# Six, then eight buffers for attention's exponentials, wo's maximum by a matrix product, wo's inputs by halves into one lasting tile, and a new order of all steps

## The chip, the cores and the metric

One core of a Trainium2 chip runs the whole program. The time is the device time of one execution in microseconds; the number compared is the median over runs. Before the change it is 800.88 us (three runs: 796.53, 800.88 and 806.01).

The core's engines work through their own instruction streams in order and meet at semaphores: PE (matrix products; PEld is its weight loading), DVE (vector), ACT (activations), POOL, and SP, which here only issues DMA transfers.

## The reference

Two independent results are joined along the last axis. A is windowed attention with 32 heads of 18 features, 2048 positions and a window of 256. B is a state-space convolution: a kernel of 2048 taps for each of 576 channels is formed from 128 complex modes, and convolved with u.

```python
def _A_ref(x, wqkv, wo):                     # x [1,2048,576]
    q, k, v = split((x @ wqkv), heads=32, Dh=18)
    scores = einsum("bhqd,bhkd->bhqk", q, k) * 18 ** -0.5
    mask = (idx[:, None] - idx[None, :] >= 0) & (idx[:, None] - idx[None, :] < 256)
    p = softmax(where(mask, scores, -1e9))
    return einsum("bhqk,bhkd->bhqd", p, v).concat_heads() @ wo

def _B_ref(u, A_re, A_im, B_re, B_im, C_re, C_im, log_dt, Dskip):
    dt = exp(log_dt)[:, None]
    P = exp((dt * A)[:, :, None] * arange(2048))      # A = A_re + 1j*A_im
    K = einsum("dn,dnl,dn->dl", Cc, P, dt * Bc).real
    return irfft(rfft(pad(u.T)) * rfft(pad(K)))[:2048].T + u * Dskip

return concatenate([a, b], axis=-1)
```

## The kernel before

**The order is a table.** Every piece of work is a Python generator (a stream) whose steps each issue a few instructions. `run` reads the strings of `PLAN` from left to right: a letter advances that stream by one step, a letter with a digit issues an evacuation, a conversion or a store that an earlier step of that stream has posted. So `PLAN` alone sets the order of instructions on every engine and on SP's queue. The conditions that the generators yield beside their steps play no part when the program is built. There are four strings: `front` (loads, scales, the first projections), `tables` (projections, the taps of B, transforms of u and of the taps), `first` (the last taps beside the first attention blocks), and `rest` (attention, convolution, output projection).

**PSUM.** All work but the projections and the products P times V takes its PSUM tile from `slot()`: the string `SLOTS` names, allocation by allocation, one of three ring buffers of two banks. A ring buffer comes free when the evacuation that reads it has run.

**Attention** has 16 items (4 chunks of 512 queries times 4 groups of 8 heads). For each item `smax1` forms the scores on PE (L901 the product, L909 and L912 the mask) and takes row maxima on DVE (L935); 16 reductions for each item. The maxima are transposed (L917, L921) and written by DMA into row 54 of Q (L928). `scores` and `score1` form the scores again, transposed, with the maximum taken off (L971, mask L984). ACT takes the exponential into an SBUF tile P of 128x2x512 (L989). `pv` multiplies P by V (L1009) into the PSUM tile `po`. An item has 5 blocks of keys, and a block needs two P tiles, so there are 160 exponentials. The pool `P` has 4 buffers: the fifth exponential waits until the products that read the first are done.

**Normalizing.** ACT copies `po` to `osb` (L1019). DVE transposes, takes reciprocals and transposes back (L1035, L1037, L1039). POOL multiplies (L1044), ACT makes the high half in f16 (L1048), POOL the low half (L1052), and SP stores both to the DRAM tensor `od` (L1057).

**The output projection.** `wo_load` fetches wo in four column pieces, reduces each to its maximum over the row (DVE L1081), then needs the maximum over all 128 partitions: `om` is stored to a row of DRAM (L1088), loaded back to all partitions as `orow` (L1090), and reduced there (L1092, result `og`). From it come the scales `so` and `osc` (L183 to L187 and L1095). `wo` loads one chunk of 512 positions at a time as f16 high and low tiles `oh` and `ol` (8 DMAs, L1117 and L1118) from a pool with one buffer each. Then come 8 groups of 14 matmuls (L203; ring tiles read woh, wol, oh and ol), and the result is scaled (ACT L1132, tile `ya`, two buffers) and stored (L1133).

**The convolution** in `rest`: loads of spectra parts (L705), forward products (L717), ACT copies (L725), DVE products (L732), POOL sums (L738, L739), inverse products (L750), stores and loads through `h` (L757, L763, L802), last products (L813) and outputs (ACT L820, store L824).

**Memory.** The pool `rawp` has 8 tiles of 128x5x256 f32. They first hold the eight pieces of x. `early` then reuses six of them as Q, K and V of the first two items; two tiles lie idle after that, and so do the two K tiles once the first two items have their scores.

Of the kernel before, what the change touches and what calls it, by code (L numbers as in the profile page):

```python
# [10 lines left out]
F32 = mybir.dt.float32  # L11
F16 = mybir.dt.float16
# [30 lines left out]
def constants():  # L43
# [23 lines left out]
    for nm, v in mult.items():  # L67
# [34 lines left out]
        "PMP6RP5XP5X4P6XG6ssM1RNX2NsssRssMss2s2X1sU4X5s2ssZss2ss2Zsss2s2XX1X4s2s2Zss2Rs2s2Xs2X5Zs2s2",
    "first":
        "Rs2ssMs6M1Rss4s2sss2X2as2aa1X4Ma1s2XRss2sXX1s2sX1sXsas2vsaX5a1s2sa1X2X4svs2as2vs2X4ssavaX4sX4a1as2ss"
        "2s2a1avs2s2sa1svsassa1s6s2s2sss2s2a1s",
    "rest":
        "s2sa1ssvvsss2vs2ss2s4ssvas2av1kss2as2as2a1s2ka1a1s2a1s2vcknvLc1s2skaLaaa1vs6a1ks4vcc2svka1lkc1slsasv"
        "kas2saa1a1s2vs2s2c2avcs2sks2sas2a1sn3a1ss2vc1sLs2vc3a1aLdv1s2Lsc3a1c2csds2d1svlsaas2kvc1c2s2cd1a1s2s"
        "sLka1d4nc3vc1s2d4ks2vaa1aslsasvas6s2svs2dLsas4a1a1svs2c2c3a1d1c3ss2sa1n1vks2aa1svasdsLss2n6a1s2vv1s2"
        "Las2svd1a1n3saslvLs2ls2ss2s2kasa1s2s2lcs2ssn1sa1s6s2das2c1a1vsLcc2d1c1vaas2nvssa1d4n6c3laks4a1sava1s"  # L110
        "s2vavss2s2a1kss2vs2vsn3s2adas2sa1csv1d4d4a1svsn4d1c2s2aa1ss2vc3s2s2ac1dss2aa1c2a1d1vvks2Lc3nsa1Ln1aL"
        "dsd4a1vkd1n3sass6s2s2va1sasn4va1d4sad4s2sa1s2vcss4s2vkLss2saaan6fsc1s2sa1vfLss2ea1s2skLs2s2vs2sas2va"
        "1c2v1s2c3ase1Lds2s2a1e4a1sls6n1ss2ssvsavksasd1ss2a1fvksaa1svaas4s2La1va1fs2kcvs2s2n4a1s2slavsc1s2s2a"
        "1asnLa1vsas2s2kaLv1s2c2vva1n6cLsa1ssleas2c1fave1vs2s2s2se4a1kaacs6a1a1vvaa1c2ss4ac1nvssLvsas2s2c3sa1"
# [1143 lines left out]
```

## Time and profile before

| what | value |
|---|---|
| median of 3 runs | 800.88 us |
| the profiled execution | 799.52 us |
| its span in the trace | 797.8 us |
| mean granted PE clock | 0.974 |
| PE busy | 693.7 us (87%) |
| DVE busy | 601.7 us (75%) |
| ACT busy | 534.1 us (67%) |
| POOL busy | 369.2 us (46%) |
| DMA | 150.74 MB, mean 189 GB/s |

Times in the trace are counted from the start of the span; 1.7 us of the execution lie outside it. The strings of `PLAN` can be told apart by which lines run: the projections end near 355 us, the taps near 387 us, the first product P times V is at 389.5 us, and the last one ends at 756.6 us. After that only the output projection and the last products of the convolution are left.

### The profile page before, as it was taken

To read this page: it belongs to the slowest core of one execution; us is meant where nothing else is said; L and a number is where in the kernel's file an instruction comes from. 1 tells how busy PE (TensorE), PEld (TensorE's weight loads), DVE (VectorE), ACT (ScalarE), POOL (GpSimd) and SP (SyncE) were. 2 spreads that over 40 slices of the span, in tenths; PEclk is the share of its full clock that TensorE was granted. 3 is DMA by queue.
4 is the path that set the end of the run, shared out by engine and by line. 5 is a ranking of instruction groups with operands and counts; after the bars stand their busy time and mean duration, and the time that the engine had idled before them with its cause. 6 is when DMAs were issued, how large, how long until landed. Compare 5 with 4: busy or idle time off the path is not lost.

```text
span 797.8 us, 29495 instructions
## 1 busy us (share of the span) xinstructions
PE 693.7 (87%) x12954; PEld 406.1 (51%) x12954; DVE 601.7 (75%) x803; ACT 534.1 (67%) x709; POOL 369.2 (46%) x285
## 2 busy tenths in 40 slices
PE   3775889988889989987888999988999998999986
PEld 2532445455445645655544555544545555466655
DVE  5898988988898898778788988867888788851010
ACT  2279677787876787773466677765777868775422
POOL 2236967886789667676022433230342242443120
PEclk9989899999999999996899999999999999999999
DMA  8978256348336727887669677778566797636574
GB/s 300 369 166 203 64 129 168 83 104 216 83 75 173 166 54 185 221 210 217 162 196 313 208 219 225 203 178 275 157 201 221 232 284 227 177 112 199 185 241 156
DMA packets 211072, 150.74 MB, mean 189 GB/s; under 512 B 103178, under 2 KB 190986, under 8 KB 210688
## 3 DMA queue, kind: packets, MB, share of 16 engines
q1 hardware_dynamic: 209328, 146.35, 64.8%
q0 software_dynamic: 1616, 2.52, 1.1%
q8 instruction: 101, 1.65, 0.9%
q14 instruction: 27, 0.22, 0.1%
HBM read 83.57 MB, written 65.11 MB: 186 GB/s over the span
## 4 chain that ended last, share of the span: by engine, by line
PE 43%; DVE 14%; ACT 13%; issue 4%; DMA 2%; SPq 2%; ACTq 0%; DVEq 0%
PE po L1009 7%; PE ring L203 7%; DVE m L935 6%; PE pp L203 5%; ACT P L989 4%; PE ring L901 4%; PE ring L971 4%; PE ring L750 3%; PE ring L717 3%; PE ring L614 2%; PE ring L813 2%; PE ring L984 1%; ACT X L725 1%; PE ring L504 1%; ACT ring L526 1%
## 5 line engine op out<-in xcount | busy, mean ns | idle before, releaser
L935 DVE TENSOR_REDUCE m<-ring 128x2 f32<-128x640 f32 (+4 forms) x256 | 189.0, 778 | 50.9 <-PE ring L909 40.9
L989 ACT ACTIVATE P<-ring,esc 128x1024 f32<-128x1024 f32 (+2 forms) x160 | 165.5, 1060 | 59.6 <-PE ring L984 52.6
L585 POOL TENSOR_TENSOR m<-A,tr 128x1024 f32<-128x1024 f32 x72 | 143.0, 2006 | 51.8 <-DVE m L591 42.9
L738 POOL TENSOR_TENSOR Y<-t,t 128x384 f32<-128x384 f32 x24 | 24.1, 1004 | 149.6 <-DVE t L732 93.5
L1044 POOL TENSOR_TENSOR osb<-osb,T 128x1024 f32<-128x1024 f32 x16 | 37.8, 2365 | 84.1 <-ACT P L989 33.3
L1009 PE MATMUL po<-P,raw 64*32 64x320 f32 (+4 forms) x1920 | 67.3, 356 | 3.2 <-issue 2.8
L591 DVE TENSOR_TENSOR m<-m,m 128x1024 f32<-128x1024 f32 x36 | 55.1, 1529 | 2.2 <-POOL m L585 2.1
L203 PE MATMUL pp<-xh,wh 128*128 128x512 f16 x180 | 47.4, 393 | 9.0 <-ACT vst L404 3.5
L909 PE MATMUL ring<-sm,idb 64*64 64x128 bf16 x896 | 54.2, 222 | 0.0
L203 PEld LDWEIGHTS <-wh 128*128 128x128 f16 x324 | 30.6, 98 | 45.2 <-issue 10.9
L614 PE MATMUL ring<-Q,m 128*32 128x64 f32 x2304 | 42.6, 230 | 11.6 <-DVE m L591 4.8
L901 PEld LDWEIGHTS <-raw 54*64 54x64 f16 x704 | 28.3, 107 | 46.7 <-issue 43.0
L1052 POOL TENSOR_TENSOR oh<-osb,oh 128x1024 f16<-128x1024 f32 x16 | 34.2, 2136 | 37.8 <-ACT oh L1048 26.7
L614 PEld LDWEIGHTS ring<-Q,m 128*32 128x32 f32 x2304 | 36.7, 116 | 25.1 <-issue 6.1
L901 PE MATMUL ring<-K,raw 54*64 54x320 f16 (+4 forms) x576 | 45.1, 309 | 4.3 <-DVE m L935 0.9
L566 POOL TENSOR_TENSOR tr<-tr,mab 128x768 f32<-128x768 f32 x18 | 33.2, 1844 | 31.2 <-ACT tr L561 31.0
L1035 DVE STREAM_TRANSPOSE T<-osb 128x1024 f32<-128x1024 f32 x16 | 19.8, 1236 | 36.7 <-ACT osb L1019 36.3
L203 PE MATMUL pp<-xh,wl 128*128 128x512 f16 x180 | 46.2, 388 | 0.0
L725 ACT ACTIVATE X<-ring 128x768 f32<-128x768 f32 x48 | 36.8, 809 | 13.3 <-PE ring L717 10.4
L732 DVE TENSOR_TENSOR t<-X 128x768 f32<-128x768 f32 x48 | 43.6, 950 | 2.1 <-POOL Y L739 2.1
L971 PEld LDWEIGHTS <-K 55*64 55x64 f16 x1280 | 29.5, 106 | 29.3 <-issue 25.9
L984 PE MATMUL ring<-tm,idb 64*64 64x256 bf16 (+2 forms) x640 | 44.3, 256 | 0.0
(163 smaller groups left out, 1633.3 us busy)
## 6 DMA issues: line engine op xcount, KB each, us to landing
gk<-kst SPq DMA_DIRECT2D x36, 256.0 KB
gx<-ust SPq DMA_DIRECT2D x16, 576.0 KB
xk<-gx SPq DMA_DIRECT2D x24, 384.0 KB
xk<-gk SPq DMA_DIRECT2D x24, 384.0 KB
h<-ho SPq DMA_DIRECT2D x48, 192.0 KB
hp<-h SPq DMA_DIRECT2D x24, 384.0 KB
K<-kz SPq DMA_DIRECT2D x14, 512.0 KB
raw<-qz SPq DMA_DIRECT2D x11, 512.0 KB
```

The lines of the kernel that those rows point to most:

```text
L203: self.nc.tensor.matmul(ps, u, v, start=(i == 0), stop=(i == len(ops) - 1))
L585: tt(m[part], A[:, ch, a0:a0 + 8].unsqueeze(3).to_broadcast(sh), tr[:, ch, part, 0:8].unsqueeze(2).to_broadcast(sh), op=OP.mult)
L591: self.nc.vector.tensor_tensor(m[0], m[0], m[1], op=OP.add)
L614: nc.tensor.matmul(kp[32 * st:32 * st + 32, j, :], m[:, ch, 32 * term:32 * term + 32], Q[:, ch, term, :], start=(term == 0), stop=(term == ...
L725: nc.scalar.activation(X[:, i], pi[i][:, :, :384], AF.Copy)
L901: nc.tensor.matmul(ps[z:z + 64, b, :n], d["Q"][rr, 2 * b + pp, 64 * qb:64 * qb + 64], d["K"][rr, 2 * b + pp, k0:k1], start=True, stop=Fals ...
L909: nc.tensor.matmul(out, self.idb[rr], self.sm[rr], start=False, stop=True, skip_group_check=True)
L935: self.nc.vector.tensor_reduce(out, x, axis=AX.X, op=OP.max)
L971: nc.tensor.matmul(ps[z:z + 64, b, off:off + w], d["K"][rr, 2 * b + pp, kc:kc + 64], d["Q"][rr, 2 * b + pp, q0:q0 + w], start=(k == 0), st ...
L984: nc.tensor.matmul(out, self.idb[rr], self.tm[rr, 64 * at:64 * at + n * w], start=False, stop=True, skip_group_check=True)
L989: nc.scalar.activation(P[:, :, lo:hi], ps[:, :, lo:hi], AF.Exp, scale=self.esc)
L1009: nc.tensor.matmul(po[32 * p:32 * p + 32, z, q0:q0 + w], V[64 * z:64 * z + 64, kb * 76 + 19 * p:kb * 76 + 19 * p + 32], P[p % 2][64 * z:64 ...
```

## The change

Four edits:

1. `ptile` replaces the allocation of P. The pool keeps its 4 buffers. The two idle tiles of `rawp`, and from the 21st exponential on the two old K tiles of the first items as well, are used in turn with them: 6 buffers for exponentials 0 to 19, 8 afterwards.
2. The maximum over partitions: `om`, read with a stride of zero, is the stationary operand of a product with the identity, so that every row of the ring tile is `om` transposed (L1097). DVE reduces straight from PSUM (L1099). The tensor `omx`, the tile `orow` and both their DMAs are gone.
3. A new stream `y` (`wo_in`) loads wo's inputs by halves of 256 positions into one `oh` and one `ol` tile that last to the end: 8 DMAs for each half, 64 in all where there were 32, of half the bytes each. The stream `w` keeps only the products.
4. All four strings of `PLAN`, and `SLOTS`, are replaced.

```diff
-        "svs2a1avs2s2sa1svsassa1s6s2s2sss2s2a1s",
+        "ss2ssa1sX4ss2sX4sssvas2s6a1X4s2s2ss2",
...
-            self.first[i].update({"Q": q, "V": raw["V"][:, 0:928], "K": Shifted(k, 256), "k": k})
+            self.first[i].update({"Q": q, "V": raw["V"][:, 0:928], "K": Shifted(k, 256), "k": k, "old": raw["K"]})
...
         self.Ps, self.osb = {}, {}
+        old = [self.p["rawp"].tile([128, 5, 256], F32, name="raw").rearrange("p a b -> p (a b)") for _ in range(2)]
+        old += [self.first[i]["old"] for i in range(2)]
+        self.pb = [x[:, 0:1024].rearrange("p (b x) -> p b x", b=2) for x in old]
...
+    def ptile(self):
+        k = self.n["P"]
+        self.n["P"] += 1
+        z = k % 6 - 4 if k < 20 else (k - 20) % 8 - 4
+        return self.p["P"].tile([128, 2, 512], F32, name="P") if z < 0 else self.pb[z]
...
-            P = self.p["P"].tile([128, 2, 512], F32, name="P")
+            P = self.ptile()
...
-        row = sp.tile([128, 128], F32, name="orow")
         yield "DVE", ()
         nc.vector.tensor_reduce(om, amx, axis=AX.X, op=OP.max)
-        yield "SP", (om,)
-        nc.sync.dma_start(self.omx.rearrange("o p -> p o"), om)
-        yield "SP", (om,)
-        nc.sync.dma_start(row, self.omx.partition_broadcast(128))
+        yield "PE", (om,), "ring"
+        row = self.slot()
+        nc.tensor.matmul(row[:, 0, 0:128], om.to_broadcast([128, 128]), self.idf, start=True, stop=True)
         yield "DVE", (row,)
-        nc.vector.tensor_reduce(og, row, axis=AX.X, op=OP.max)
+        nc.vector.tensor_reduce(og, row[:, 0, 0:128], axis=AX.X, op=OP.max)
...
+    def wo_in(self):
+        wp = self.p["wo2"]
+        self.oh = oh = wp.tile([128, 5, 512], F16, name="oh")
+        self.ol = ol = wp.tile([128, 4, 512], F16, name="ol")
+        for c in range(4):
+            for u in range(2):
+                yield "SP", (), lambda: self.ndone >= 4 * c + 4
+                n = slice(256 * u, 256 * u + 256)
+                for z in range(2):
+                    for i, t in ((0, oh), (1, ol)):
+                        o = self.od[c, :, i, z, n]
+                        self.nc.sync.dma_start(t[:, 2 * z:2 * z + 2, n], o[0:256].rearrange("(k p) n -> p k n", p=128))
+                        self.nc.sync.dma_start(oh[64 * i + 32 * z:64 * i + 32 * z + 32, 4, n], o[256:288])
+
     def wo(self):
...
-            yield "SP", (), lambda: self.ndone >= 4 * c + 4 and self.wready
-            oh = wp.tile([128, 5, 512], F16, name="oh")
-            ol = wp.tile([128, 4, 512], F16, name="ol")
-            for z in range(2):
-                for i, t in ((0, oh), (1, ol)):
-                    nc.sync.dma_start(t[:, 2 * z:2 * z + 2], self.od[c, 0:256, i, z].rearrange("(k p) n -> p k n", p=128))
-                    nc.sync.dma_start(oh[64 * i + 32 * z:64 * i + 32 * z + 32, 4], self.od[c, 256:288, i, z])
+            oh, ol = self.oh, self.ol
...
-            self.omx = dp.tile([1, 128], F32, name="omx")
...
-                      "l": self.wo_load(), "w": self.wo()})
+                      "l": self.wo_load(), "y": self.wo_in(), "w": self.wo()})
```

In the rows of order below, the brackets name the semaphores for which an instruction waits (DMAHW for a transfer); equal rows in sequence are one row with a count.

Lines behind the edits move by 3 to 14: L901 is now L904, L935 is L938, L971 is L980, L984 is L993, L989 is L998, L1009 is L1018, L1019 is L1028, L1117 and L1118 are L1127 and L1128, L1132 is L1146.

**The maximum of wo on DVE**, in the middle of `rest`. First the order before: `og` stands behind nine of attention's reductions and waits for a DMA.

```order
L1039 STREAM_TRANSPOSE T<-R 128x1024 [waits DVE_49]
L935 TENSOR_REDUCE m<-ring 128x2 [waits PE_49] x9
L1092 TENSOR_REDUCE og<-orow 128x1 [waits DMAHW6_49]
L183 TENSOR_SCALAR og<-og 128x1 [waits DVE_49]
L184 TENSOR_SCALAR op<-og 128x1 [waits DVE_49]
L186 RECIPROCAL or<-op 128x1 [waits DVE_49]
L187 TENSOR_SCALAR or<-or 128x1 [waits DVE_49]
L1095 SCALAR_TENSOR_TENSOR osc<-pz,op 128x1
L935 TENSOR_REDUCE m<-ring 128x2 [waits PE_49] x6
```

The same place on DVE after the change.

```order
L1048 STREAM_TRANSPOSE T<-R 128x1024 [waits DVE_49]
L938 TENSOR_REDUCE m<-ring 128x2 [waits PE_49] x4
L1099 TENSOR_REDUCE og<-ring 128x1 [waits PE_49]
L183 TENSOR_SCALAR og<-og 128x1 [waits DVE_49]
L184 TENSOR_SCALAR op<-og 128x1 [waits DVE_49]
L186 RECIPROCAL or<-op 128x1 [waits DVE_49]
L187 TENSOR_SCALAR or<-or 128x1 [waits DVE_49]
L1102 SCALAR_TENSOR_TENSOR osc<-pz,op 128x1
L938 TENSOR_REDUCE m<-ring 128x2 [waits PE_49] x10
```

`og` stands five reductions earlier among the item's maxima, and it waits for PE instead of a DMA. `om` still stands some 18 DVE instructions ahead of it.

**The last loads of wo's inputs on SP.** First the order before: the load of the last chunk, one group of 8 (two `oh` or `ol` tiles of 512 positions and the 32-row remainders), behind the stores of the last item.

```order
L1057 DMA od<-oh_13382 18x2048 [waits DMAHW3_49]
L1133 DMA out_dram<-ya 128x576 [waits DMAHW4_49]
L1133 DMA out_dram<-ya 128x576 [waits DMAHW5_49,Activation_49]
L1117 DMA oh<-od 128x2x512 [waits DMAHW2_49,DMAHW1_49,DMAHW6_49,DMAHW0_49,PE_49]
L1118 DMA oh<-od 32x512 [waits DMAHW7_49,DMAHW3_49]
L1117 DMA ol<-od 128x2x512 [waits PE_49]
L1118 DMA oh<-od 32x512
```

The same place on SP after the change: the eight DMAs of the last chunk's first half, the two outputs behind them, and the first DMA of its second half.

```order
L1147 DMA out_dram<-ya 128x576 [waits DMAHW3_49,Activation_49]
L1127 DMA oh<-od 128x2x256 [waits DMAHW4_49,PE_49]
L1128 DMA oh<-od 32x256 [waits DMAHW5_49,PE_49]
L1127 DMA ol<-od 128x2x256 [waits DMAHW6_49,PE_49]
L1128 DMA oh<-od 32x256 [waits DMAHW7_49]
L1127 DMA oh<-od 128x2x256 [waits DMAHW0_49]
L1128 DMA oh<-od 32x256 [waits DMAHW1_49]
L1127 DMA ol<-od 128x2x256 [waits DMAHW2_49,PE_49]
L1128 DMA oh<-od 32x256 [waits DMAHW3_49]
L1147 DMA out_dram<-ya 128x576 [waits DMAHW4_49,Activation_49]
L1147 DMA out_dram<-ya 128x576 [waits DMAHW5_49,Activation_49]
L1127 DMA oh<-od 128x2x256 [waits DMAHW6_49,PE_49]
```

Each half now waits for the products that read the same half of the chunk before. On PE the tail moves too: behind the last product P times V stood 112 matmuls of L203 for chunk 2, then 112 for chunk 3, with three groups of L813 (two of them between the chunks). Now 56 of chunk 1, 112 of chunk 2 and 112 of chunk 3 stand there, with two groups of L813 inside chunk 2 and one between chunks 2 and 3.

**Exponentials on ACT**, near the end of `rest`. First the order before: the exponentials of the last items.

```order
L1132 ACTIVATE ya<-ring,osc 128x576 [waits PE_49]
L989 ACTIVATE P<-ring,esc 128x1024 [waits Activation_49]
L1048 ACTIVATE oh_12666<-osb 128x1024 [waits DMAHW2_49,DMAHW1_49,DMAHW7_49,DMAHW0_49,Pool_49]
L989 ACTIVATE P<-ring,esc 128x1024 [waits PE_49,Activation_49]
L1132 ACTIVATE ya<-ring,osc 128x576 [waits PE_49]
```

ACT after the change, the same part of the program; `raw` names the P tiles that lie in the old buffers.

```order
L1146 ACTIVATE ya<-ring,osc 128x576 [waits DMAHW5_49,PE_49]
L998 ACTIVATE P<-ring,esc 128x1024
L998 ACTIVATE raw<-ring,esc 128x1024 [waits PE_49] x2
L1146 ACTIVATE ya<-ring,osc 128x576 [waits DMAHW4_49,PE_49]
L1028 ACTIVATE osb<-po 128x1024 [waits Pool_49]
```

Counted along the strings, the number of P tiles in use just after an exponential was never above 4 and 2.40 on average over the 160; now it is 3.05 on average, above 4 for 20 of the 160, and 6 at the most.

More of the change, by code (lines that the diff above doesn't have):

```diff
@@ L102 @@
[L102 removed]
+        "GMGGPGG1GG5G6G2PP1PP2PM1G5G6NMP1G5GP2G1MNG5G6P4PG2M1P1P2G6RNP4UPPGMP1RMP2XRM1PX1MPG1G2GGMG5RG6G5PP1X"
+        "PG6P4PX1XM1UGPNMX5P4RRRX2PGPNGUG1MU2X4P2U1P1RXG5G2XP4UNG6M1X1X1MP2U4G5G6U2PPMRRXPU1P1PM1X4MXX5P2PNMG"
+        "X1UGX2PRPG1P1PM1RG5PNXX1GUG5P1G2RPP2MMXG6P4U2P2PU1P4GG6RM1PX5MPMX4GP1P4RPPNG5P2XPX2U4X4G1M1P4RX1XG6X"
+        "1P1G2PP4XP1X5MP2GMG5NPPGM1G6X2PRPP2PNRP4P4MPMP1RPG1P2RXG2M1X4GP4P1UXPP2X1NG5MX4PX1U4GP1G6G5P2X4UU2MG"
@@ new lines @@
+        "6RRPXU1PX4PUM1NXX2P1U4RMPPGNX5P2PG1P4PX1MP4PGPM1RP5XX1XP5GUPG2PPMURG5X4G6PX5G5X2MG6RNPU2UU1RM1XP4PU2"
+        "P5PPMGP5NPPMRX1RU1UPG1P6PP5PM1PUG2U1MGXPMPG5GP5PPU2U4RG6X1GXM1MG5G6P5PPRNX4RPX2PG1G2P6X4MX5XM1X4MGP5"
+        "PPGX1MPXG5NG6P1X4P2RG5G6PM1P1X1XNRP2PPPGX2MX5PMP1G1URXPP4GX1RPP2GG2M1P6P4PNRPMG5MG5P1X4G6M1P1P2XG6PX"
+        "1XP4PNP2GG1X2PRPPP1X5RX4MXMUG2PP4U4X1P6RX4M1U2MGU1MXPP1U4GPUPP4UPG5NPP2M1X1P2G5P4PXRG6G6RPNPX4RP1U1M"
+        "X5P2MP4GP1U2X4XNPX2M1UPG1RP2P5U4XPX4UMG2GU2PPPX1X1GG5P5G6U1PG5RMP5M1PPPPG6XRX4PMPXP4URPNGGU4P5RMX1X5"
@@ new lines @@
+        "PPX2PG1M1XG2PPU4NP4PX4GP5X4MPP5G5X1XG5PG6RP5GG6PX5RX2MM1P5PNRMNPPXPX1PP1MPP2G1RPRM1P6G2UPMP1UGX4XUU1"
+        "X4MU2G5PGG6PX1PP2M1G5U1P4U2G6XP4RP1PPP2PUNMPGP1U4X5G1URRNPMU1P1X2XP2M1U2GPPX1G5PGP2G2P1G5P4MMPPG6M1X"
+        "G6NPX1P1U4P2PX4PRRXUP4MRXMZX4PX2P4PPP2P1M1X5X1RP1P6P4UGPNMP2MP6U1X4M1XX1P4G1P2P6PGX4PG5U2MP5PPUU4PU4"
+        "PXPRGG2RPPG6P5X5UG5G6UU2ZPUPNMPPXRGPX2P5U1ZU1M1P5RG1U2MPX1PG2MXPP5M1X1MPGNP4G5PRG6P5PU4P4PGMPG5PXRM1"
+        "P6U4RXP5G6sP5P6sP6NsX2P6sRX4X5ssMss2ss2ss2X4s2s2s2s2s2s2ZNssX1s2sZsRs2ss2Xss2X4sX1Xs2ZRZs2s2",
@@ new lines @@
+        "2a1Lc1vs2avac2a1sva1csc3as2kslva1s2a1c1svs2s2sa1kadsc3vcsds2sav1a1d1kc1d1c2kLs2vd4lla1LLs2c2ss2acss2"
+        "sd4ans2vn3lvaa1s2Lc1aa1skssva1s6ass4c3kssa1an1a1s2Lvkvs2c3dss2a1vs2d1svc2aas2sd4vs2sLa1sdLsvs2a1s2v1"
+        "s2d1asan3ss2d4lkvc3sksa1aa1s2s2s2s2vs2scn6ls2ssaa1c1la1ds6cvan4d1s4c1aa1s2vssva1vc2n1c3nsss2avsn6s2a"
+        "n3sa1vLasks2s2lsa1s2a1vsadsa1Las2d4s2s2vs2c2Ld1csa1v1s2d4vsss2s2vac1s2c2ac3Lc3a1a1n4dsas2ss2kadvksas"
+        "d1a1vvsaka1d1ns6n3d4ss2vs2aa1sks2d4ss2vs4ssLa1s2va1cs2ss2asfs2s2sn1vsafssc1Ls2n6ss2as2La1s2n1va1asLe"
@@ L142 @@
+    "0120120120210210120120120121021201201201201021020120120121021021021021201201201201201201201202102012"
+    "0120120102102102012012021021021021020120120120210210120120120121020121021021021021021021021021012012"
+    "0102120210120120120120120210120120120120120120120120120210210212010210210210210210210212010212012010"
+    "2102102102102102102012012012012012010210210210120121201210210210210210210210210210210120122100102102"
+    "101202012012020210202102102"
 )
@@ L160, in __init__ @@
         self.loaded = self.maxed = self.ndone = 0
-        self.n = dict.fromkeys(("fac", "pha", "sin", "ab", "prod", "add", "mg", "q", "taps", "kq", "max", "Y", "h"), 0)
+        self.n = dict.fromkeys(("fac", "pha", "sin", "ab", "prod", "add", "mg", "q", "taps", "kq", "max", "Y", "h", "P"), 0)
     def pool(self, es, name, bufs, space=None, side=None):
```

69 lines of the change are left out of this document (22 added, 47 removed).

## The prediction

> **What bounds the kernel now.** I read the share of busy time by stage first. The columns are the stretch, its length, then busy time of PE, PEld, DVE, ACT and POOL with instruction counts, the granted PE clock, the DMA share and GB/s.
>
> ```profile
> 0.00:62.00 62.00, 38.04 (x143) 21.56 (x144) 50.65 (x57) 25.80 (x34) 17.35 (x22) 0.94 0.89 276
> 62.00:350.00 288.00, 255.15 (x3375) 145.55 (x3373) 247.88 (x339) 221.51 (x356) 214.93 (x169) 0.98 0.57 140
> 350.00:410.00 60.00, 48.07 (x1136) 31.55 (x1136) 50.25 (x79) 28.66 (x40) 18.48 (x16) 0.83 0.77 203
> 410.00:757.00 347.00, 320.23 (x8065) 184.64 (x8059) 250.07 (x328) 248.26 (x270) 113.95 (x78) 1.00 0.70 210
> 757.00:798.00 41.00, 32.23 (x248) 22.78 (x244) 2.85 (x3) 9.89 (x13) 4.48 (x2) 1.00 0.61 199
> ```
>
> From 410 us on PE is the bound: 92% busy, while DVE and ACT are at 72%. In the tail (757 on) it is PE and what PE waits for. From 62 to 350 us PE and DVE are close (89% and 86%) and work is handed round between four engines. The change adds and removes almost no PE work, so it can win only what PE loses: idle time and a lowered clock. From 410 to 757 that is 347.00 - 320.23 = 26.8 us of idle time, in the tail 8.8 us, of which the last 4.3 are the last output's way out.
>
> Next come the waits, who for whom: total, times, longest.
>
> ```profile
> PE ring L901 <- DVE m L935: 7.6, 15, 3.5
> ...
> PE ring L614 <- DVE m L591: 4.8, 1, 4.8
> PE ring L971 <- ACT P L989: 4.1, 11, 0.9
> ...
> PE ring L203 <- DMA oh<-od: 2.5, 2, 1.3
> ...
> PE ring L901 <- ACT P L989: 1.3, 4, 0.4
> ...
> ACT P L989 <- PE po L1009: 5.8, 9, 1.1
> ```
>
> Two single waits are large, 3.5 and 4.8 us, and only the first touches an edit. The chain of work that ended last has it too (start, length, what):
>
> ```profile
> 535.05 4.99 DMA orow<-omx
> 540.04 0.02 issue
> 540.06 0.30 DVE og L1092
> ```
>
> **The change part by part**, against the profiled execution of 799.52 us.
>
> *wo's maximum.* In order of time, DVE and PE near 540 us; the bracket is idle time before the row and what ended it.
>
> ```profile
> 540.06 0.29 DVE L1092 TENSOR_REDUCE og<-orow 128x1 f32<-128x128 f32 x1 [3.83 <-DMA orow<-omx]
> ...
> 541.10 2.28 DVE L935 TENSOR_REDUCE m<-ring 128x2 f32<-128x640 f32 x3
> ...
> 541.97 0.33 PE L901 MATMUL ring<-K,Q 54*64 54x320 f16 x4 [3.54 <-DVE m L935]
> ```
>
> DVE stood 3.83 us for the DMA. The reductions queued behind `og` hold ring buffers, so PE stood 3.54 us. The load was late because SP's queue reached it only at 535.05. Afterwards the clock was down:
>
> ```profile
> 541.00:543.00 2.00, 1.03 (x24) 0.37 (x23) 2.00 (x5) 0.00 (x0) 0.00 (x0) 0.83 1.12 361
> 543.00:545.00 2.00, 2.00 (x44) 1.10 (x29) 1.20 (x3) 0.00 (x0) 0.00 (x0) 0.50 1.06 333
> 545.00:547.00 2.00, 2.00 (x73) 1.26 (x72) 2.00 (x4) 1.49 (x2) 0.00 (x0) 0.81 1.11 362
> ```
>
> PE's busy time there times the clock it lacked is 1.03 x 0.17 + 2.00 x 0.50 + 2.00 x 0.19 = 1.55 us. Both losses go with the two DMAs. In comes one product, whose nearest row is the transposition of the maxima (also 128 f32 columns):
>
> ```profile
> L917 PE MATMUL ring<-idf,m 128*32 128x128 f32 x14 | 4.0, 282 | 0.6 <-ACT P L989 0.6
> ...
> DVE m L921 <- PE ring L917: 11.0, 11, 2.2
> ```
>
> That is 0.28 us on PE. Its ring buffer is held until `og` (0.29 us) runs. `og` can still make DVE wait, now for PE: the second row, DVE behind that transposition, bounds this between 0 and 2.2 us. I take 0: four reductions stand between, and PE forms their inputs first anyway. What is late next is attention's own reduction, as everywhere in this stage. Term: 3.54 + 1.55 - 0.28 = **4.8 us** gained (bounds 2.6 to 4.8).
>
> *wo's inputs by halves.* The tail on PE, last chunk:
>
> ```profile
> 755.61 1.09 PE L1009 MATMUL po<-P,raw 64*32 64x320 f32 x28 [0.27 <-ACT P L989]
> ...
> 759.50 0.28 PE L203 MATMUL ring<-woh,oh 128*128 128x288 f16 x1 [0.77 <-issue]
> ...
> 775.29 1.51 PE L813 MATMUL ring<-hp,i 128*64 128x384 f32 x8 [0.96 <-ACT y L820]
> 776.73 0.42 PE L203 MATMUL ring<-woh,oh 128*128 128x288 f16 x2
> 778.36 0.42 PE L203 MATMUL ring<-woh,oh 128*128 128x288 f16 x2 [1.21 <-DMA oh<-od]
> 780.09 0.28 PE L203 MATMUL ring<-woh,oh 128*128 128x288 f16 x1 [1.31 <-DMA oh<-od]
> ...
> 792.83 0.65 PE L203 MATMUL ring<-woh,ol 128*128 128x288 f16 x4
> ```
>
> The load of chunk 3 starts only when chunk 2's last matmul has run, since both use one buffer:
>
> ```profile
> 766.63 1.67 SPq L1057 DMA_DIRECT2D od<-oh  x4
> 768.35 0.84 SPq L1133 DMA_DIRECT2D out_dram<-ya  x2
> 772.43 0.38 SPq L1117 DMA_DIRECT2D oh<-od  x1
> ...
> 776.76 0.46 SPq L1118 DMA_DIRECT2D oh<-od  x1
> ```
>
> The eight issues take 772.43 to 777.22, and PE is fed at 780.09, so a load takes up to 7.7 us. After the change a half's load waits for a half chunk: 56 matmuls. A chunk's 112 take 13.4 us here (780.09 to 793.5), a half 6.7. Behind a half's release stand the other half (6.7 us) and, for chunk 3, one group of L813 (1.5 us): 8.2 us of cover against at most 7.7. The last item's store ended at 768.3, 11.7 us after the last product P times V; now 56 + 56 matmuls and two groups of L813 (16.4 us) stand before the release that chunk 3's first load needs, so the release and not the store comes last. Chunk 2's second half is covered by 6.7 + 2 x 1.5 us. Queued behind each waiting load on SP are outputs, the last loads of `hp` and the next half; nobody but ACT's two `ya` buffers waits for these outputs, and PE runs two ring buffers ahead of them. So 1.21 + 1.31 go, and the 0.96 with the chunk boundary at which L813 met a full ring. Term: **3.5 us** (bounds: 0 if the cover fails by 0.5 to 3 us on both halves, 4.3 if the 0.77 us at 759.50 goes too).
>
> The 32 added DMAs cost SP 32 x 0.46 = 15 us of issuing. This is hidden, since SP mostly waits for data; two of its largest waits:
>
> ```profile
> SPq L480 <- PE ring L492: 39.1, 7, 11.6
> ...
> SPq L763 <- ACT ho L757: 23.0, 10, 5.0
> ```
>
> Uncovered, one group of eight costs 4.8 us. The Trainium skill speaks against this edit: "DMA: Bandwidth & Descriptors", section "Measured (HBM→SBUF, 128 partitions, SWDGE, issued from GpSimd)", would have transfers batched to 1 MiB or more and calls those under 64 KB dominated by descriptors; these fall from 256 and 32 KB to 128 and 16. By its fixed 2 us for a DMA, 32 more in series would be 64 us. In the trace eight of them land within 7.7 us of the first issue, so they overlap, and the sum goes by that row.
>
> *More P buffers.* The exponentials as a group (busy time, mean ns; then ACT's idle time ahead of them):
>
> ```profile
> L989 ACT ACTIVATE P<-ring,esc 128x1024 f32<-128x1024 f32 (+2 forms) x160 | 165.5, 1060 | 59.6 <-PE ring L984 52.6
> ```
>
> ACT waited for `po` 5.8 us in nine exponentials. PE waits for an exponential's ring buffer 4.1 + 1.3 us in the rows above. More buffers remove the first wait; of the second they remove only what follows from it, since most of it is the 1.1 us that an exponential takes. At 20 of 160 exponentials more than four buffers are in use. Bounds 0 and 5.4; I take **2.0**, nearer to 0, because ACT's 5.8 us are idle time of an engine that is 72% busy. The borrowed tiles were last used long before; nothing is waited for.
>
> *The order.* The front up to 62 us keeps its rows on DVE, its busiest engine; 0. Elsewhere all four strings are new. Nothing in the trace prices that. The nearest unit is the change of stages:
>
> ```profile
> 362.00:374.00 12.00, 10.41 (x204) 7.20 (x207) 11.69 (x20) 1.30 (x4) 9.88 (x11) 0.50 0.99 294
> 374.00:388.00 14.00, 10.47 (x267) 7.52 (x261) 8.05 (x15) 5.87 (x7) 2.70 (x2) 0.72 0.39 65
> ```
>
> There the clock cost 10.41 x 0.50 + 10.47 x 0.28 = 8.1 us. A new order can win one such stretch or make one: 0, bounds -8.1 and +8.1. The PE order around it has the same groups in nearly the same sequence, so I expect it to stay. The Trainium skill ("TensorE: Matmul & The Clock Gate", Part 1: The HAM clock gate) has the clock return after one busy window of about 3.4 us. By it such a stretch would cost at most 1.7 us and the new order hardly anything. The trace disagrees: the clock stays at 0.50 for 12 us with PE 87% busy, so the rows set the bounds.
>
> *Sum:* 4.8 + 3.5 + 2.0 = 10.3; 799.52 - 10.3 = 789.2. The profiled execution lies 1.4 us under the median of the runs, so I predict **790 us**.
>
> **Rivals.**
> - *Given back:* the local waits go, but PE meets others in their place (a ring buffer held by a reduction or an ACT copy). For it: many PE waits here are under 1 us and spread over all engines, and the old order had been broken only where a transfer was late. Against it: the tail has nothing left to wait for. Then only the tail's 3.5 us stay: 797.
> - *Clock regained:* the new order closes the idle time ahead of 362 us, and the 8.1 us go as well: 782. Against it stands the similar sequence.
> - *Slower, taps behind the sums:* in `tables` PE waits for DVE's sum L591, which waits for POOL's products. Before, one wait of 4.82 us in the 36 groups of taps. If three more taps meet it, each costs 4.82 and the clock as after 541 us, 1.55: 3 x 6.4 = 19.1, 790 + 19 = 809. From the second one on the gain is gone (12.7 against 10.3). For it: POOL is 75% busy there with a chain of products and sums, and its order is new; against it, one in 36.
> - *SP becomes the bound:* the 15 us of added issuing stand on the path, because a load that waits for PE holds up SP's queue: 790 + 15 = 805. For it: SP reached `orow` late because it stood before other transfers. Against it: the groups stand where 6.7 us of matmuls cover them. The Trainium skill's rule on small transfers, named above, is the case for this rival.
> - *The change doesn't do what it says:* if a half's load waits for the whole tile, the tail keeps its 3.5 us, 793.5; this joins the first rival.
>
> **How the numbers follow.** Forecast 50%, given back 32% (the last rival included), clock regained 11%, taps 5%, SP 2%. A measurement of this kernel tells about 1% from no change: under 792.8 is faster. The forecast lies there but for a tenth, clock regained wholly: 0.45 + 0.11 = 0.56 faster; slower 0.06 (taps, and a little of SP's case), same 0.38. The range takes the clock's case at the bottom (781), and at the top "given back" with part of the order's loss: 802.
>
> **What would show it.** `og` with under 2.2 us of idle time before it, and no halved clock behind it; no wait of L203 for `oh<-od` in the last 30 us; the wait of exponentials for `po` near 0, and PE's for exponentials 1 to 3 us less; the clock between 360 and 388 us as before. The prediction is wrong if PE's idle time from 62 to 757 us, with the clock's loss, changes by over 8 us for other reasons than these.

## The result

| kernel | median, us | runs | lowest to highest |
|---|---|---|---|
| before | 800.16 | 20 | 795.48 to 806.88 |
| after | 793.66 | 20 | 785.63 to 798.22 |

The ratio is 0.9928, with a 95% interval of 0.9907 to 0.9949. By the medians this is 6.5 us less, by the interval 4.1 to 7.4. The prediction was 790, with a range of 781 to 802 that held the result. The execution of after that was profiled took 797.37 us, one of the slowest of the 20, with a mean granted clock of 0.964; that of before took 799.52 with 0.974. So the two traces differ by 2.2 us where the medians differ by 6.5, and a second profiled execution of after (794.19 us, below "after, second") stands beside the first where it matters.

The stretches of after, columns as before (length, then busy PE, PEld, DVE, ACT, POOL, clock, DMA, GB/s):

```profile
62.00:350.00 288.00, 253.61 (x3327) 145.62 (x3330) 241.10 (x339) 221.65 (x354) 212.10 (x164) 0.98 0.57 140
350.00:410.00 60.00, 46.98 (x1074) 31.25 (x1063) 47.20 (x75) 26.26 (x40) 21.81 (x20) 0.80 0.70 177
410.00:757.00 347.00, 323.72 (x8175) 187.86 (x8168) 259.59 (x338) 253.72 (x273) 115.52 (x79) 0.99 0.71 216
757.00:795.60 38.60, 34.34 (x268) 24.88 (x265) 0.00 (x0) 9.94 (x13) 4.15 (x2) 1.00 0.67 201
```

PE's idle time from 410 to 757 us fell from 26.8 to 23.3, in the tail from 8.8 to 4.3. From 350 to 410 the clock fell from 0.83 to 0.80 and PE was busy for 1.1 us less, so the change lost there.

The maximum of wo on PE and DVE in after. Nothing in brackets stands at `og` (no idle time ahead of it); DVE runs through, and PE idled 0.40 us ahead of the product:

```profile
535.15 0.49 PE L1097 MATMUL ring<-idf,om 128*128 128x128 f32 x2 [0.40 <-DVE m L938]
```
```profile
534.27 1.56 DVE L938 TENSOR_REDUCE m<-ring 128x2 f32<-128x640 f32 x2 [0.17 <-PE ring L912]
535.74 0.28 DVE L1099 TENSOR_REDUCE og<-ring 128x1 f32<-128x128 f32 x1
```

The tail on PE: in the last 38.6 us one row has idle time ahead of it, and no wait for `oh<-od` is left. The second row is the last product.

```profile
778.29 0.28 PE L203 MATMUL ring<-woh,oh 128*128 128x288 f16 x1 [0.33 <-issue]
...
791.02 0.65 PE L203 MATMUL ring<-woh,ol 128*128 128x288 f16 x4
```

The waits of after that answer to those of before (total, times, longest):

```profile
PE ring L614 <- DVE m L591: 5.3, 1, 5.3
...
PE ring L904 <- DVE m L938: 4.1, 14, 0.4
...
PE ring L904 <- ACT P L998: 3.1, 5, 1.2
...
ACT P L998 <- PE po L1018: 1.8, 1, 1.8
...
PE ring L904 <- ACT raw L998: 1.7, 5, 0.7
...
PE ring L980 <- ACT P L998: 0.6, 2, 0.3
...
PE ring L980 <- ACT raw L998: 0.5, 1, 0.5
```

So the long wait at `og`, the waits for `oh<-od` and most of ACT's wait for `po` are gone. PE's waits for the exponentials' ring buffers, where 1 to 3 us less were expected, are not smaller: 4.1 + 1.3 = 5.4 us before, 5.9 here (`raw` is an exponential in a borrowed tile) and 6.3 in the second profile. The wait for L591 stayed, 5.3 us where it had been 4.8.

The change of stages got worse. The same two stretches as in the prediction, and the two behind them:

```profile
362.00:374.00 12.00, 8.20 (x211) 5.82 (x210) 11.76 (x21) 3.92 (x8) 8.62 (x11) 0.65 0.95 212
374.00:388.00 14.00, 9.71 (x213) 6.62 (x207) 9.52 (x16) 5.46 (x6) 4.21 (x2) 0.62 0.69 173
388.00:400.00 12.00, 10.53 (x320) 7.03 (x312) 7.38 (x11) 5.61 (x9) 0.00 (x0) 0.94 0.46 99
400.00:412.00 12.00, 9.01 (x225) 4.76 (x218) 9.43 (x18) 3.44 (x5) 0.00 (x0) 0.86 0.72 232
```

In the kernel before the last two had the full clock:

```profile
388.00:400.00 12.00, 10.35 (x299) 6.04 (x294) 8.84 (x15) 7.30 (x9) 0.00 (x0) 1.00 0.76 224
400.00:412.00 12.00, 9.72 (x253) 4.91 (x248) 10.47 (x15) 6.56 (x7) 2.04 (x1) 1.00 0.70 222
```

In the two stretches that the prediction priced the clock cost no more than its 8.1 us: 6.6 here and 8.1 in the second profile. What grew is PE's idle time there and the clock's cost behind 388 us.

PE's loss can be summed by stage: idle time, and busy time multiplied by the clock it lacked, in slices of 5 us. What is left of the span is PE's work at full clock.

| loss, us | 0 to 350 | 350 to 425 | 425 to 725 | 725 to the end | all | work |
|---|---|---|---|---|---|---|
| before | 62.9 | 21.8 | 25.0 | 9.9 | 119.6 | 678.2 |
| after | 67.1 | 26.0 | 24.0 | 4.2 | 121.4 | 674.2 |
| after, second | 65.7 | 26.2 | 21.7 | 4.2 | 117.9 | 674.5 |

The change won 1 to 3 us in the attention stage and 5.7 at the end, and lost 3 to 4 us up to 350 and 4.3 at the change of stages. PE's work fell by 3.8 us for the same products; no group of instructions shows where, and some records are missing from every trace, so this part stays open.

### The profile page after: what moved, and what is told of

It reads as the page before. It is cut to its first block, busy times and chain, and to the rows that moved or that the text cites. A ratio compares the mean times of both kernels' runs of the same rounds, so it can differ in the third digit from the quotient of the medians.

```text
span 795.6 us, 29497 instructions
## 1 busy us (share of the span) xinstructions
PE 697.2 (88%) x12956; PEld 411.0 (52%) x12956; DVE 596.1 (75%) x803; ACT 535.1 (67%) x709; POOL 370.7 (47%) x285
## 4 chain that ended last, share of the span: by engine, by line
PE 37%; DVE 7%; ACT 6%; issue 3%; DMA 3%; SPq 1%; POOL 1%; ACTq 0%; POOLq 0%; DVEq 0%
PE po L1018 8%; PE ring L203 7%; PE ring L904 4%; DVE m L938 4%; PE ring L980 3%; PE ring L750 3%; PE ring L717 3%; PE ring L813 2%; ACT raw L998 2%; ACT P L998 1%; PE ring L993 1%; PE ring L912 1%; ACT X L725 1%; PE ring L614 1%; DMA raw<-qz 1%
## 5 line engine op out<-in xcount | busy, mean ns | idle before, releaser
L938 DVE TENSOR_REDUCE m<-ring 128x2 f32<-128x640 f32 (+4 forms) x256 | 188.9, 778 | 53.6 <-PE ring L912 41.3
L998 ACT ACTIVATE P<-ring,esc 128x1024 f32<-128x1024 f32 (+2 forms) x86 | 89.8, 1059 | 38.7 <-PE ring L993 36.7
L998 ACT ACTIVATE raw<-ring,esc 128x1024 f32<-128x1024 f32 (+2 forms) x74 | 77.0, 1061 | 22.8 <-PE ring L993 22.3
L203 PEld LDWEIGHTS <-wh 128*128 128x128 f16 x324 | 31.3, 101 | 46.4 <-issue 13.4
L203 PE MATMUL pp<-xh,wh 128*128 128x512 f16 x180 | 48.6, 400 | 6.4 <-DVE xh L384 3.6
L904 PEld LDWEIGHTS <-raw 54*64 54x64 f16 x704 | 28.7, 108 | 48.1 <-issue 43.4
L591 DVE TENSOR_TENSOR m<-m,m 128x1024 f32<-128x1024 f32 x36 | 51.4, 1428 | 0.3 <-POOL m L585 0.2
L904 PE MATMUL ring<-K,raw 54*64 54x320 f16 (+4 forms) x576 | 44.9, 308 | 7.0 <-ACT raw L998 1.7
L203 PE MATMUL pp<-xh,wl 128*128 128x512 f16 x180 | 46.7, 391 | 0.8 <-DVE wl L371 0.8
L993 PE MATMUL ring<-tm,idb 64*64 64x256 bf16 (+2 forms) x640 | 44.3, 257 | 0.0
L526 ACT ACTIVATE ring<-ring 128x1024 f32<-128x1024 f32 x36 | 36.7, 1019 | 9.0 <-PE ring L504 8.1
L980 PEld LDWEIGHTS <-K 55*64 55x64 f16 x1280 | 28.9, 106 | 26.7 <-issue 23.1
```

Source lines behind the costliest of these rows:

```text
L203: self.nc.tensor.matmul(ps, u, v, start=(i == 0), stop=(i == len(ops) - 1))
L591: self.nc.vector.tensor_tensor(m[0], m[0], m[1], op=OP.add)
L904: nc.tensor.matmul(ps[z:z + 64, b, :n], d["Q"][rr, 2 * b + pp, 64 * qb:64 * qb + 64], d["K"][rr, 2 * b + pp, k0:k1], start=True, stop=Fals ...
L938: self.nc.vector.tensor_reduce(out, x, axis=AX.X, op=OP.max)
L980: nc.tensor.matmul(ps[z:z + 64, b, off:off + w], d["K"][rr, 2 * b + pp, kc:kc + 64], d["Q"][rr, 2 * b + pp, q0:q0 + w], start=(k == 0), st ...
L993: nc.tensor.matmul(out, self.idb[rr], self.tm[rr, 64 * at:64 * at + n * w], start=False, stop=True, skip_group_check=True)
```

## The experiments

The first question was whether the edits or the new order made the gain. The strings of `PLAN` can be exchanged at the seams of the stages, so both can be had nearly alone. "Old" and "new" below mean the strings of before and of after; line numbers of these kernels are up to 12 lower than after's. Each ratio is to the kernel before, run in turn on the same chip; each median is over 6 to 12 runs.

| kernel | front, tables | first | rest | edits | median, us | ratio (95%) |
|---|---|---|---|---|---|---|
| after, second | new | new | new | all | 793.84 | 0.9899 (0.9860 to 0.9939) |
| edits, old order | old | old | old | all | 798.99 | 0.9962 (0.9936 to 0.9987) |
| old early, new rest | old | old | new | all | 789.37 | 0.9818 (0.9769 to 0.9866) |
| the same again | old | old | new | all | 789.35 | 0.9854 (0.9818 to 0.9889) |
| new early, old rest | new | new | old | all | 805.68 | 1.0051 (1.0023 to 1.0079) |
| old tables, new first | old | new | new | all | 795.00 | 0.9918 (0.9882 to 0.9954) |
| product alone | old | old | old | product | 797.19 | 0.9956 (0.9927 to 0.9985) |
| buffers alone | old | old | old | buffers | 800.92 | 1.0008 (0.9976 to 1.0040) |
| maximum by DMA | new | new | new | all but product | 800.74 | 0.9991 (0.9958 to 1.0023) |
| whole loads | new | new | new | all but halves | 812.63 | 1.0146 (1.0104 to 1.0189) |
| late chunk 0, old early | old | old | new | all | 789.19 | 0.9862 (0.9824 to 0.9899) |
| late chunk 0, new | new | new | new | all | 793.64 | 0.9907 (0.9871 to 0.9943) |

### The three edits in the old order

```diff
  PLAN, SLOTS of before, in rest:
- l (store om)  ...  l (load orow)  L n3 d s2 s2 s s     s2 s2  l (og)
+                                   L n3 d s2 s2 s s  l  s2 s2  l (og)
  wo(): both halves' 16 loads where the chunk's 8 loads stood
```

> The three edits (exponentials' buffers, maximum by a product, halves) in the old order of steps; only the steps for the maximum are moved, the product to the place just ahead of its reduction. Theory A, the edits bring the gain and the new order gives part of it back: 789 to 791 us, faster than the changed kernel (793.7) by 3 to 4 us; no wait of PE behind og and none for oh in the last 30 us. Theory B, the edits bring the gain and the order nothing: 793 to 794. Theory C, the order brings the gain and the edits at most a local microsecond or two: 798 to 800, near the kernel before (800.2).

The median is 798.99 us, theory C's figure: in the old order the edits together bring 0.4%. Near `og` PE's wait of 3.54 us has become three of 1.94 us together, with the full clock behind them, but the halves gained nothing at the end. PE in the tail of this kernel; brackets as before:

```profile
770.33 1.51 PE L810 MATMUL ring<-hp,i 128*64 128x384 f32 x8 [1.49 <-ACT ya L1139]
...
780.87 0.77 PE L200 MATMUL ring<-woh,oh 128*128 128x288 f16 x5 [2.76 <-ACT ya L1139]
```

PE no longer waits for `oh<-od`, it waits 4.25 us for ACT's copies into `ya`. ACT and SP show why:

```profile
780.08 0.74 ACT L1139 ACTIVATE ya<-ring,osc 128x576 f32<-128x576 f32 x1 [6.69 <-DMA out_dram<-ya]
```
```profile
768.48 0.38 SPq L1124 DMA_DIRECT2D oh<-od  x1
...
776.89 0.47 SPq L1125 DMA_DIRECT2D oh<-od  x1
777.46 8.18 SPq L1140 DMA_DIRECT2D out_dram<-ya  x5
```

All 16 loads of a chunk stand in SP's queue ahead of the outputs of the chunk before. The queue goes on to the outputs only at 777.46 us, `ya` has two buffers, and so ACT, then the ring, then PE stand still. Both halves' loads stand together in every kernel that has them with the old `rest`; a place of its own for the second half in the old order was not tried.

### The new order in rest, and in what comes before

```diff
  PLAN, for "old early, new rest" (front, tables and first of before)
- rest: "s2s4s2vvvkvs..."
+ rest: "s2sa1" + "s2s4s2vkvs..."  (two v, one a with its a1 out; s, s2, a1 in)
  PLAN, for "new early, old rest" (front, tables and first of after)
- rest: "s2sa1ssvv..."
+ rest: "vvaa1ssvv..."
```

> The changed kernel with the old order in front, tables and first (to about 410 us), the new one in rest; at the seam one score step, two products P times V and one row maximum are exchanged. Theory A, with the loss put into the change of stages at 350 to 425 us (first product P times V at 393.0 us instead of 389.5): 789 to 791 us, first product P times V at 389 to 390 us. Theory B: 793 to 794 wherever the early part stands. Theory C: most of the new order's gain is in rest: 793 to 795.

> The three edits, the new order in front, tables and first, the old one in rest, with the same exchange at the seam. Theory A: 3 to 4 us over the edits in the old order throughout, 793 to 794, the first product P times V at 392 to 394 us. Theory B: the same as the edits in the old order, 793 to 794, but the first product at 389 to 390 us or the difference made up behind it. Theory C: 798 to 802.

> The changed kernel once more, for a second profiled execution beside the first one, which at 797.4 us was among the slowest of its runs. All theories: 793 to 795 us. If the late first product P times V (393.0 us) and the clock of 0.78 to 0.86 at 375 to 425 us belong to the order, they are there again; if they belong to that execution, the first product is at 388 to 390 us.

Of the four combinations with all edits, old-old took 798.99, old-new 789.37, new-old 805.68 and new-new 793.84. The new order of rest is worth 9.6 us behind the old beginning and 11.8 behind the new one; the new beginning costs 4.5 us ahead of the new rest and 6.7 ahead of the old. Theory A had the sign of the beginning and its place right, and the first product P times V is about where it put it: at 392.8 us in the second profile of after and 392.6 with the new beginning and the old rest, at 388.6 and 390.8 in the two profiles of the old beginning with the new rest. (The maximum by DMA, with the new beginning, has it at 389.6 all the same.) But the edits don't make the gain by themselves, as A and B had it, the gain of rest is larger than C's, and 805.68 is above what any of the three gave for that kernel. Part of the gain of rest shows on PE in the last stretch, from 725 us to the end: first the edits in the old order, then the old beginning with the new rest.

```profile
725.00:795.20 70.20, 59.81 (x678) 41.80 (x675) 2.85 (x3) 24.08 (x29) 8.48 (x4) 1.00 0.63 195
```
```profile
725.00:790.20 65.20, 61.33 (x734) 44.39 (x722) 5.69 (x6) 28.52 (x33) 11.32 (x6) 1.00 0.72 219
```

PE is idle for 10.4 us in the first and 3.9 in the second. In the new rest outputs stand between the half loads, and no wait for `ya` is left on PE. So 6.5 of the 9.6 us lie in the tail, and 4.25 of them are waits for `ya`: this part of the order is the place that it gives to the second half's loads, and can't be told from the third edit. Of the rest of the 9.6 us these profiles show 3.3 us less of PE's work and no gain from 425 to 725 (22.4 and 25.2 us lost); the two profiled executions differ by 5.0 us only, so the traces don't hold the remainder.

### Which string of the beginning costs the time

```diff
  PLAN, front and tables of before, first and rest of after
- first: "sRss6ss4..." with two X5
+ first: "Rs2" + "sRss6ss4..." with one X5, ring buffers 0, 1, 2 renamed 1, 2, 0
```

> The changed kernel with the old order in front and tables alone, the new one in first and rest (at the seam one R, one s2 and one X5 are exchanged, ring buffers renamed in first). With the old order in first too it took 789.4 us, without it 793.7. If the new tables cost the time (3 us lost by 350 us, and the clock falls there): 789 to 790.5. If first costs it (the clock and idle time at 375 to 425 us): 792.5 to 794.

The median is 795.00 us, above the 792.5 to 794 given for `first`, and far from the 789 to 790.5 given for `tables`. So the cost lies in `first`, with what its seam exchanges. From 350 to 425 us the loss is 25.3 to 27.3 us in six of the seven profiles with the new `first` (23.8 in the seventh), and 21.8 to 23.0 in six of the seven with the old one (26.4 in the seventh). What the new `first` does differently shows in the second profile of after:

```profile
401.18 0.28 PE L920 MATMUL ring<-idf,m 128*32 128x128 f32 x1 [1.27 <-DVE m L938]
```
```profile
374.00:388.00 14.00, 10.11 (x179) 7.29 (x171) 7.69 (x14) 5.15 (x6) 3.67 (x2) 0.50 0.59 138
388.00:400.00 12.00, 10.45 (x296) 6.95 (x290) 7.55 (x11) 5.73 (x9) 0.00 (x0) 0.92 0.48 97
400.00:412.00 12.00, 9.06 (x217) 4.67 (x218) 9.28 (x18) 3.29 (x5) 0.00 (x0) 0.86 0.71 250
```

The clock stays at half through 374 to 388 us, where before it had 0.72, and is lowered once more around a wait for the row maxima at 401. From 374 to 388 us it is 0.50 to 0.62 in six of the seven profiles with the new `first` (0.76 in the seventh), and 0.71 to 0.76 in all seven with the old one. The wait of this transposition for the maxima, 1.0 to 1.3 us, is in all seven of the first kind and in none of the others; but the old `first` with the new rest has waits of 0.6 and 1.3 us for maxima there too, and keeps the full clock in two of its three profiles. Which step of `first` brings the lowered clock was not tried.

### Single edits

```diff
  old_max_by_product: before, with the product alone (as in the first experiment)
  old_more_buffers:   before, with
- P = self.p["P"].tile([128, 2, 512], F32, name="P")
+ P = self.ptile()
```

> The kernel before with the product for the maximum alone, put just ahead of its reduction; nothing else is changed. If the term of 4.8 us holds: 795.5 to 797 us against 800.5 to 801.5 before, no halved clock at 536 to 546 us. Rival, the lowered clock only moves to the next idle place of PE (near 556 us, as with all three edits in the old order): 798 to 799.5.

> The kernel before with the exponentials' buffers alone (6, then 8). If the term of 2.0 us holds: 798.5 to 799.5 against 800.5 to 801.5 before. Rival, ACT's waits for po go but PE gets nothing, since DVE and PE set the pace: 800 to 802. PE's wait for the exponentials' ring buffers tells: 4.1 us before, about 2 with the gain.

The product alone brought 4.2 us by the medians (797.19 against 801.38, just above the 795.5 to 797 of its term); the ratio of 0.9956 makes it 3.5, with an interval of 1.2 to 5.9. PE around it, in a profiled execution near the slowest of its runs (801.27 us):

```profile
543.00 0.49 PE L1085 MATMUL ring<-idf,om 128*128 128x128 f32 x2 [0.52 <-ACT ho L754]
...
543.88 0.41 PE L968 MATMUL ring<-raw,K 55*64 55x320 f16 x8 [0.38 <-DVE og L1087]
...
545.45 0.33 PE L898 MATMUL ring<-K,Q 54*64 54x320 f16 x4 [1.05 <-DVE m L932]
```

The single wait of 3.54 us has become three of 1.95 us together, and in this execution the clock was still halved from 546 to 549 us behind them, which the 4.8 had counted as gone; in after, and in the edits in the old order with the same three waits, it was not. DVE waited 2.1 us for the product here, nearly the 2.2 that the prediction gave as the bound.

The buffers alone brought nothing that can be measured (800.92, ratio 1.0008); the interval runs from 1.9 us less to 3.2 more and leaves the 2.0 just outside. ACT's 5.8 us of waits for `po` are gone from its list, and PE's waits for the exponentials fell only a little, from 4.1 + 1.3 us:

```profile
PE ring L980 <- ACT P L998: 1.9, 6, 0.6
...
PE ring L980 <- ACT raw L998: 1.4, 3, 0.9
...
PE ring L904 <- ACT raw L998: 0.6, 2, 0.4
...
PE ring L904 <- ACT P L998: 0.4, 2, 0.2
```

(The four are 4.3 us together.) The new order has up to six exponentials' buffers in use at a time, so what four would cost it was not tried.

The other way round, one edit undone in the new order:

```diff
  new_max_by_dma: after, with
- nc.tensor.matmul(row[:, 0, 0:128], om.to_broadcast([128, 128]), self.idf, start=True, stop=True)
+ nc.sync.dma_start(self.omx.rearrange("o p -> p o"), om)
+ nc.sync.dma_start(row, self.omx.partition_broadcast(128))
  new_whole_loads: after, with the 8 DMAs of a chunk of 512 behind the last product of the chunk before
```

> The changed kernel with the maximum over partitions again by the two DMAs over DRAM, the store some 25 steps behind om and the load where the product stood. If the term of 4.8 us for the maximum holds in the new order: 797 to 799 us (changed kernel 793.7), with PE idle 2 to 4 us behind og and a clock of 0.5 for some 4 us after it. Rival, the wait depends on where SP stands, and in the new order the load is in time: 793.5 to 795, PE idle under 1 us there.

> The changed kernel with wo's inputs again by whole chunks into one tile, all eight DMAs behind a chunk's last matmul. If the tail term of 3.5 us holds: 796.5 to 798.5 us, with two or more waits of L203 for oh in the last 30 us. Rival, the halves only turn the wait for oh into one for the outputs' tiles ya, as they did in the old order (2.8 us): 793 to 795.

Without the product the kernel took 800.74 us, 7 more than after, as the first theory had it and above its range. But the trace is the rival's:

```profile
  DMA orow<-omx: 0.6, 1
who waited for it (us, times):
  DVE og L1098: 0.6, 1
```

DVE waited 0.6 us and PE not at all. In this profile (798.91 us) the clock is halved in two places, from 560 to 567 and from 676 to 683 us, and 27.2 us are lost from 425 to 725 against after's 24.0 and 21.7. The first place lies behind a wait of 1.14 us for the maxima in Q, which the last experiment is about, the second behind 2.27 us for which the profile names no cause. That the two DMAs in SP's queue bring this about is not shown; where the 7 us lie stays open.

Without the halves it took 812.63 us, 19 more than after and far above the 796.5 to 798.5 expected. The new order starts each chunk's products soon after the chunk before, and a whole load can't keep up:

```profile
PE ring L200 <- DMA oh<-od: 11.6, 6, 2.6
```
```profile
725.00:815.20 90.20, 72.09 (x776) 48.27 (x768) 5.69 (x6) 29.84 (x35) 14.30 (x7) 0.90 0.52 160
```

PE is idle for 18.1 us in the last stretch, where after has 4.2, and the clock falls to 0.90 with it. So the new order is made for the halves, and this loss is not what the halves would bring to the old one.

### A better place for chunk 0's loads

In six of the eight profiles of kernels with the halves PE waits 0.3 to 1.3 us between 556 and 561 us for a store of maxima, which it does in no profile without them. First PE of "old early, new rest", then SP:

```profile
557.21 0.98 PE L977 MATMUL ring<-Q,K 55*64 55x64 f16 x12 [0.84 <-DMA Q<-m]
```
```profile
546.41 0.72 SPq L1124 DMA_DIRECT2D oh<-od  x1
...
552.30 0.46 SPq L1125 DMA_DIRECT2D oh<-od  x1
...
553.33 3.03 SPq L928 DMA_DIRECT2D Q<-m  x4
```

The second half of chunk 0 takes SP 6.35 us of issuing (546.41 to 552.76) ahead of that store, though the chunk is used only near 705 us. Both half loads were moved to where SP is idle.

```diff
  PLAN, rest
- d4 n6 L y c3 k e4 s6 y f s4 ...
+ d4 n6 L c3 k e4 s6 f s4 ... s6 y n6 s4 ...  l y d4 ...
```

> Old order to about 410 us and new order in rest, and the two half loads of wo's chunk 0 moved from the 16 issues ahead of a store of maxima (L928, about 555 us) to two idle stretches of SP, near 590 and 670 us; the chunk is used only near 705 us. Theory D, the added issues hold up that store, PE waits for Q, and the clock falls behind it: no wait of PE for Q<-m near 557 us, no halved clock at 556 to 566 us, 785 to 787.5 us against 789.4 without the move. Rival, the clock falls there in any case (DVE's reductions and the exponentials are late as well): 789 to 791.

> The changed kernel with the same move of chunk 0's two half loads. Theory D: the 1.0 to 1.3 us wait for Q<-m near 561 us goes, and a lowered clock where one followed: 791 to 793 against 793.7. Rival: 793.5 to 794.5, since no lowered clock was seen at this place in the changed kernel's two profiles.

> The old order to about 410 us with the new one in rest once more, beside the run with the moved loads. All theories: 788.5 to 791 us, with a wait for Q<-m of about 1 us near 557 us.

The wait went as theory D had it, and so did the lowered clock. Before the move, and after it:

```profile
558.00:562.00 4.00, 3.48 (x76) 1.69 (x72) 2.38 (x3) 2.12 (x2) 1.41 (x1) 0.56 1.00 301
562.00:566.00 4.00, 4.00 (x60) 1.81 (x52) 2.48 (x3) 2.14 (x2) 0.00 (x0) 0.59 1.03 361
```
```profile
558.00:562.00 4.00, 3.38 (x96) 1.96 (x99) 3.30 (x6) 2.37 (x3) 2.12 (x2) 1.00 0.96 295
562.00:566.00 4.00, 3.78 (x68) 1.67 (x72) 2.85 (x4) 3.21 (x4) 0.00 (x0) 1.00 0.98 307
```

The median did not move: 789.19 against 789.35, and 793.64 against 793.84 with the new beginning. With the old beginning theory D's 785 to 787.5 lie just below the interval (787.8 to 793.8); with the new one its 791 to 793 overlap it (791.6 to 797.3). In the profile after the move with the old beginning the clock falls at 538 us instead, yet from 425 to 725 us both profiles lose less than those without the move: 20.3 us against 25.2 and 25.3, and 19.5 against 24.0 and 21.7 with the new beginning. So theory D is right on the place, and its gain in time is not shown; six runs each can't tell 2 us from none. The best version stays the old beginning with the new rest, 789.4 us: 1.5 to 1.8% under before, 0.5% under after.

## Why the prediction was right, and where its working was not

- **wo's maximum, 4.8 us: right in size; the mechanism is shown in part.** Alone it brought 4.2 (1.2 to 5.9). In after the stall and the halved clock behind it went, and `og` had no idle time; alone, in the old order, part of both stayed in the one profile. Taken back out of the new order it cost 7 us, though `og` then waited only 0.6 us: that loss is not the wait that the term is made of.
- **wo's inputs by halves, 3.5 us: right in after, but tied to the place of the loads.** In after no wait for `oh<-od` is left, and PE's idle time from 757 us on fell by 4.5 us (8.8 to 4.3), a little over the upper bound of 4.3. The step "nobody but ACT's two `ya` buffers waits for these outputs, and PE runs two ring buffers ahead of them" holds there and failed with the edits in the old order, where PE waited 4.25 us through `ya`. The edit and the order of rest earn the gain together: without the halves the same order loses 19 us. The rival on SP (2%) told the old order right in kind.
- **More buffers, 2.0 us: mis-sized.** Alone they brought 0, the lower bound. ACT's wait of 5.8 us went wholly and PE's by 1.1 of 5.4, and the time did not follow; in after PE's did not fall at all.
- **The order, 0: wrong.** It is two parts of opposite sign, about -9.6 in rest (the place of the half loads included) and +4.5 in `first` (with all edits; -11.8 and +6.7 by the other path). The sentence that failed is "The PE order around it has the same groups in nearly the same sequence, so I expect it to stay": the loss from 350 to 425 us rose from 21.8 to 26.0 and 26.2, of it idle time by about 2 us and the clock's part by 2.1 to 2.6.
- **The rivals.** "Given back" (797) is nearest to the traces in kind, since the beginning loses what the end wins; by the time the result lies halfway between it and the forecast. Its place was not a ring buffer in attention but the change of stages. "Clock regained" did not come, since the two stretches cost 6.6 and 8.1 us of clock, and neither did the taps behind L591's sums: it is one wait, 5.3 us instead of 4.8. The prediction gave 0.56 to a result under 792.8, which was not reached, and 0.38 to "same", under which 793.66 falls.
- **By the prediction's own test the working is wrong.** PE's idle time and clock loss from 62 to 757 us, in the same slices, are 84.7 us before, 89.9 in after and 87.7 in its second profile: 5.2 and 3.0 more, where the terms for `og` and the buffers asked for 6.8 less. So 12.0 and 9.8 us came for other reasons, where 8 was the limit.
- **That 790 is near 793.7 is luck in good part.** The sum of the edits is 10.3 us (from the median it gives 790.6); in the old order they brought 2.5, with an interval of 1.0 to 5.1. The order, 0 in the sum, brought the rest: a gain in rest and a loss in `first` that largely cancelled.

## What to carry to other kernels

When a change also brings a new order, run the edits in the old order and exchange the order stage by stage: here the parts were -10 and +5 us, larger than any single edit in the old order, and a combination beat both kernels. Splitting the loads helped here only where the outputs that free `ya` did not stand behind both halves in the same queue; look at what the queue issues next, not only at the cover. A wait that is taken away is not time won until the median says so: the buffers and the moved loads both removed real waits and brought nothing that the medians show.

## What was not expected of the hardware

The clock after a short stall is not the same from one profile to the next. Near `og` the product alone and the edits in the old order have the same three waits of 1.95 and 1.94 us, and only the first lost the clock behind them. Around the wait for `Q<-m` PE was busy much alike in two kernels; in the second profile of after the clock stayed, with the old beginning it was halved:

```profile
558.00:560.00 2.00, 1.33 (x55) 0.80 (x48) 2.00 (x4) 1.12 (x1) 2.00 (x2) 1.00 0.42 125
560.00:562.00 2.00, 1.10 (x32) 0.86 (x36) 0.58 (x1) 0.00 (x0) 2.00 (x2) 1.00 0.84 215
```
```profile
556.00:558.00 2.00, 1.14 (x20) 0.62 (x23) 1.40 (x2) 0.10 (x1) 2.00 (x2) 1.00 0.27 43
558.00:560.00 2.00, 1.48 (x48) 1.13 (x44) 0.83 (x1) 1.59 (x2) 1.41 (x1) 0.62 0.90 263
560.00:562.00 2.00, 2.00 (x40) 0.56 (x35) 1.56 (x2) 0.53 (x1) 0.00 (x0) 0.50 1.10 339
```

The Trainium skill ("TensorE: Matmul & The Clock Gate", Part 1: The HAM clock gate) says that the activity window runs freely, so that the moment of a change varies between runs of one kernel. The traces agree in that it varies, and show no window: in two executions of "old early, new rest" the clock cost 8.0 and 13.2 us from 350 to 425 us. A term for a lowered clock is therefore a term with a chance, and one profile doesn't price it.
